# Windowed attention and a gated feed-forward in one kernel: which engine issues the transfers of results

## The chip, the cores and the metric

One core of one Trainium2 chip runs the whole program. The metric is the device time of one execution in microseconds (us), lower is better; the median of three runs stands for the kernel, and one further execution was taken with a profile.

## What is computed

Eight batches, eight heads, 512 local and 32 global positions, head size 64; then a feed-forward over 544 rows of 512 numbers per batch, with 1024 hidden ones:

```
out_g = softmax(q_g [k_g,k_l]^T / 8) [v_g,v_l]             # 32 global queries see everything
out_l = softmax(q_l [k_g, k_l where |i-j|<=32]^T / 8) [v_g,v_l]
x     = [out_g, out_l], heads side by side                  # 8 x 544 x 512
h     = max(x w_in, 0);  c = conv of 3 taps along the rows of h
out   = (h * sigmoid(c)) w_out
```

All inputs are float32 (the weights arrive as 64-bit numbers and are split on the chip into a high and a low part; x and the gated h are split too, and three products replace one).

## The kernel before

**Attention.** Heads go in pairs. `LQ` and `LV` load a pair's queries, keys and values (704 and 448 KB), `LG` the global queries. `SC` (line 258) makes the scores on TensorE in two PSUM banks, `MA` (286, 287) masks them and takes the maximum on VectorE, `EX` (299) exponentiates on ScalarE, `NP` normalizes, `TD` (309) transposes on VectorE, `PV` (350) multiplies by the values into four PSUM banks, and `UA` (205) copies these on ScalarE into a tile `nt`. Line 205 is the helper `cp` for every copy, line 208 the helper `sub` for every difference. The global queries run through `G`, `GM`, `GE`, `GS`, `GT`, `GC`, `GP` (436) and `GO`, which copies the result on ScalarE into a tile `og`.

**The row.** Results go to DRAM and come back in another shape: `XW` (line 361) writes `nt` into a DRAM tensor `row`, `GW` (448) writes `og` there, and `XR` (368) reads a piece of the row, 486 to 488 columns of one of four quarters of x, into a tile `xl`. `XH` (205, ScalarE) rounds it into `xh`, and `XL` (208, VectorE in the first chunk, GpSimd later) leaves the rest in `xl`. A piece needs every `XW` and `GW` whose columns lie in it.

**Feed-forward.** The row is cut into nine chunks (`CUTS`). For each, `Z` (466) makes eight tiles `ps_h` of hidden numbers, `RE`, `C1`, `C2`, `TH`, `GG`, `GH`, `GL` make the gate on ScalarE and VectorE, and `O` (520) makes four output tiles in `ps_o`. `OE` (205) copies one into a tile `o`, on ScalarE in the first chunk and on VectorE from the second on, and `ST` (534) stores it; where a chunk reaches over the end of a batch, `ST` is two transfers.

**Weights.** `WD` (168) loads eight pieces `raw` of 1 MB, and `WA` (107, ScalarE), `WC` (114 to 118 and 192, VectorE), `WH` (205, ScalarE), `WL` (208, VectorE) turn each into its two parts.

**Order.** A planner (`plan`, `arranged`) runs at build time: it has a cost and a due time for each operation and lists the operations in the order in which it would start them; `emit` records them in that order and ties each engine to it. So each engine, and each engine's queue of transfers, works strictly in the planner's order. In the planner's list of engines (`FIXED`, line 658) every transfer stands under SyncE (SP), and all are issued there. PSUM has eight banks for everything (`SLOTS["ps"]`), `nt`, `og` and `o` have two tiles each, `qk` four and `vf` six.

**Semaphores of transfers.** The framework deals eight semaphores, DMAHW0 to DMAHW7, in turn to the transfers of the whole program, whoever issues them. A transfer first waits for the landing of the last one that had its semaphore (where no other wait already covers that), so it waits for the eighth transfer before it.

Of the kernel before, what the change touches and what calls it, by code (L numbers as in the profile page):

```python
# [21 lines left out]
SL = 512  # L22
# [42 lines left out]
def attn_moe(ctx: ExitStack, tc: tile.TileContext, qk_d, vw_d, qg_d, w_in_d, w_out_d, cw_d, out_d):  # L65
    nc = tc.nc
# [24 lines left out]
    for b in range(4):  # L91
        rows = slice(b * SG, (b + 1) * SG)
        for k, sign in ((0, 1), (1, -1)):
            nc.gpsimd.affine_select(
                out=mask[rows, :, k], in_=mask[rows, :, k], pattern=[[0, 4], [sign, SG]], compare_op=ALU.is_ge, fill=NEG,
# [7 lines left out]
    row = dram.tile([NCT, P, NCOL], F32, name="row", bufs=1)  # L103
# [107 lines left out]
    heads = {}  # L211
# [146 lines left out]
    def XW(n):  # L358
        b, h = divmod(n, H)
        at = 1 + ROW * b + SG  # L360
        nc.sync.dma_start(out=row[h // 2, :, at : at + SL], in_=heads[n]["nt"])

    def XR(i):
        c, ct = divmod(i, NCT)
# [80 lines left out]

    def GW(n):
        at = ROW * (n // H)
        nc.sync.dma_start(
            out=row[:, :, at : at + 1 + SG].rearrange("c p q -> p c q"), in_=ogs[n // H % SLOTS["og"]]
        )  # L450

# [77 lines left out]
    def ST(o):  # L529
        c, mt = divmod(o, NCT)  # L530
        for b in range(B):
            lo, hi = max(CUTS[c], ROW * b), min(CUTS[c + 1], ROW * b + S)
            if lo < hi:
                nc.sync.dma_start(
                    out=out_d[b, mt, :, lo - ROW * b : hi - ROW * b], in_=outs[o][:, lo - CUTS[c] : hi - CUTS[c]]
                )

    emit(tc, B, dict(
        LQ=LQ, LV=LV, LG=LG, G=G, S=SC, M=MA, NM=NM, E=EX, NS=NS, NP=NP, TD=TD, P=PV, UA=UA, XW=XW, XR=XR,
        XH=XH, XL=XL,  # L540
        GM=GM, GE=GE, GN=GN, GS=GS, GT=GT, GC=GC, GP=GP, GO=GO, GW=GW,
        PZ=Z, RE=RE, C1=C1, Ca=lambda u: C2(u, 0), Cb=lambda u: C2(u, 2), TH=TH, GG=GG, GH=GH, GL=GL,
        Oa=lambda o: O(o, 0), Ob=lambda o: O(o, 1), OE=OE, ST=ST, WD=WD, WA=WA, WC=WC, WH=WH, WL=WL,
    ), phase)

# [431 lines left out]
```

## Time and profile before

| | us |
|---|---|
| runs (three) | 571.13, 573.1, 573.7 |
| median | 573.1 |
| the profiled execution, its own time | 569.44 |
| span of its instructions | 567.6 |

| engine | busy us | share of the span |
|---|---|---|
| TensorE, matmuls | 528.4 | 93% |
| TensorE, weight loads (beside the matmuls) | 442.8 | 78% |
| VectorE | 431.4 | 76% |
| ScalarE | 377.5 | 67% |
| GpSimd | 65.1 | 11% |

SP computes nothing. The time splits into two parts: until about 120 us weights are prepared, the first two batches' attention is made and TensorE has gaps; from there on TensorE is busy without a gap until the last chunk. The chain of work that ended last runs 82% of its length over TensorE and 11% over VectorE. Shares of the whole span hide this, so the stretches are to be read one by one.

### The profile page before, as it was taken

What the parts mean: (1) busy time and instruction counts of PE and PEld (TensorE: products, weight loads), DVE (VectorE), ACT (ScalarE), POOL (GpSimd) and SP (SyncE); (2) the same over time, 40 slices, a digit from 0 to 9 for tenths busy, and PEclk for the clock granted to TensorE, in tenths of its full rate; (3) what the DMA queues carried; (4) which work ended last, traced back from release to release, by engine and by line L of the source; (5) the groups of instructions that cost most, each with busy time, mean ns of one, the idle gap of its engine ahead of it and who ended that gap; (6) DMA issues with size and microseconds to landing.
All of it is one profiled execution on the core that took longest, in us unless ns stands there. A gap on an engine that the chain in (4) does not pass through costs nothing.

```text
span 567.6 us, 19439 instructions
## 1 busy us (share of the span) xinstructions
PE 528.4 (93%) x8208; PEld 442.8 (78%) x8208; DVE 431.4 (76%) x876; ACT 377.5 (67%) x1258; POOL 65.1 (11%) x73
## 2 busy tenths in 40 slices
PE   5574589889999999999999999999999999999997
PEld 4463468678888888888888888888888888888886
DVE  4889999987886798479847994699578873783771
ACT  4855787769974997399739973898489642441530
POOL 3400220110002001200120002000200040010000
PEclk9676689899999999999999999999999999999999
DMA  8879452464255333632464246333501321111001
GB/s 349 337 220 405 186 209 62 120 212 160 75 154 152 111 110 118 187 140 74 157 166 149 91 131 186 122 121 108 146 20 38 109 92 35 36 35 54 19 0 70
DMA packets 34982, 74.73 MB, mean 132 GB/s; under 512 B 9808, under 2 KB 21584, under 8 KB 33872
## 3 DMA queue, kind: packets, MB, share of 16 engines
q1 hardware_dynamic: 34896, 73.50, 39.0%
q8 instruction: 64, 1.05, 0.8%
q14 instruction: 22, 0.18, 0.1%
HBM read 55.65 MB, written 17.84 MB: 129 GB/s over the span
## 4 chain that ended last, share of the span: by engine, by line
PE 82%; DVE 11%; DMA 3%; ACT 2%; issue 2%; SPq 0%; ACTq 0%; DVEq 0%
PE ps_o L520 34%; PE ps_h L466 31%; PE ps_v L350 7%; PE ps_s L258 5%; PE go L436 3%; DVE negm L287 2%; DMA qgf<-qg 1%; DVE t L485 1%; DVE pt L309 1%; PE gt L421 1%; PE psg L280 1%; DVE ps_s L286 1%; DVE t L496 1%; DMA qk<-qk 1%; DVE wt L118 1%
## 5 line engine op out<-in xcount | busy, mean ns | idle before, releaser
L520 PE MATMUL ps_o<-g,w_out 128*128 128x484 f32 (+1 forms) x864 | 200.2, 385 | 2.1 <-ACT pgt L205 2.1
L466 PE MATMUL ps_h<-xh,w_in 128*128 128x486 f32 (+1 forms) x576 | 190.9, 395 | 1.5 <-ACT xh L205 1.5
L520 PEld LDWEIGHTS ps_o<-g,w_out 128*128 128x128 f32 x864 | 161.6, 189 | 30.8 <-issue 2.4
L466 PEld LDWEIGHTS ps_h<-xh,w_in 128*128 128x128 f32 x576 | 110.7, 192 | 22.8 <-ACT xh L205 2.6
L485 DVE SCALAR_TENSOR_TENSOR t<-h,cw,t 128x484 f32<-128x484 f32 (+1 forms) x144 | 105.9, 742 | 16.2 <-ACT t L238 15.6
L466 PE MATMUL ps_h<-xl,w_in 128*128 128x486 f32 (+1 forms) x288 | 112.1, 389 | 5.2 <-DVE xl L208 5.2
L299 ACT ACTIVATE pr<-ps_s,negm 128x128 f32<-128x128 f32 x256 | 90.3, 369 | 0.8
L208 POOL TENSOR_TENSOR xl<-xl,xh 128x486 fp32r<-128x486 f32 (+1 forms) x32 | 43.2, 1353 | 349.2 <-ACT xh L205 349.2
L474 ACT ACTIVATE h<-ps_h 128x486 f32<-128x486 f32 (+1 forms) x72 | 41.5, 577 | 46.1 <-PE ps_h L466 41.4
L350 PEld LDWEIGHTS ps_v<-pt,vf 32*64 32x64 f32 x3328 | 50.7, 140 | 20.8 <-issue 12.2
L466 PEld LDWEIGHTS ps_h<-xl,w_in 128*128 128x128 f32 x288 | 55.3, 192 | 14.3 <-DVE xl L208 6.0
L350 PE MATMUL ps_v<-pt,vf 32*64 32x64 f32 (+3 forms) x3328 | 56.6, 254 | 9.2 <-issue 4.4
L496 DVE SCALAR_TENSOR_TENSOR t<-t,h 128x484 f32<-128x484 f32 (+1 forms) x72 | 51.0, 713 | 16.5 <-ACT t L492 15.5
L492 ACT ACTIVATE t<-t 128x484 f32<-128x484 f32 (+1 forms) x72 | 43.8, 609 | 27.4 <-DVE t L485 27.4
L322 ACT ACTIVATE pr<-pr,sums 128x128 f32<-128x128 f32 x192 | 60.1, 404 | 0.6 <-DVE sums L316 0.5
L286 DVE TENSOR_TENSOR ps_s<-ps_s,mask 128x256 f32<-128x256 f32 x64 | 26.8, 418 | 38.8 <-PE ps_s L258 38.6
L238 ACT ACTIVATE t<-h,cw 128x484 f32<-128x484 f32 (+1 forms) x72 | 50.5, 703 | 4.8 <-DVE g L208 4.2
L299 ACT ACTIVATION_READ_ACCUMULATOR pr<-ps_s,negm 128x1 f32 x256 | 53.1, 208 | 0.0
L258 PE MATMUL ps_s<-qk 64*32 64x128 f32 x2048 | 39.6, 298 | 14.0 <-DMA qk<-qk 11.8
L309 DVE STREAM_TRANSPOSE pt<-pr 128x512 f32<-128x512 f32 x64 | 44.4, 701 | 10.4 <-ACT pr L322 9.9
L208 DVE TENSOR_TENSOR g<-t,g 128x484 fp32r<-128x484 f32 (+1 forms) x72 | 49.6, 692 | 1.4
L258 PEld LDWEIGHTS ps_s<-qk 64*32 64x32 f32 x2048 | 32.2, 114 | 21.6 <-issue 7.4
(63 smaller groups left out, 414.5 us busy)
## 6 DMA issues: line engine op xcount, KB each, us to landing
qk<-qk SPq DMA_DIRECT2D x32, 704.0 KB, 5.5
vf<-vw SPq DMA_DIRECT2D x32, 448.0 KB, 4.0
row<-nt SPq DMA_DIRECT2D x32, 256.0 KB, 3.8
xl<-row SPq DMA_DIRECT2D x24, 243.0 KB, 3.3
raw<-w_in SPq DMA_DIRECT2D x4, 1024.0 KB, 12.3
raw<-w_out SPq DMA_DIRECT2D x4, 1024.0 KB, 9.9
xl<-row SPq DMA_DIRECT2D x8, 244.0 KB, 3.1
out<-o SPq DMA_DIRECT2D x4, 242.0 KB, 3.5
```

What stands on the lines that cost most here:

```text
L208: eng(key).tensor_tensor(out=out, in0=in0, in1=in1, op=ALU.subtract)
L238: nc.scalar.activation(out=out, in_=in_, func=AF.Copy, scale=by)
L258: nc.tensor.matmul(heads[n + j]["s"][b * SG : (b + 1) * SG, t].rearrange("p (a b k) -> p a b k", a=2, b=2), lhsT=qk[rows, at : at + SG], r ...
L299: nc.scalar.activation(out=st["p"][:, t, :], in_=st["s"][:, t, :], func=AF.Exp, scale=SCALE, bias=st["m"][:, t : t + 1], accum_out=two["r" ...
L309: nc.vector.transpose(out=st["pt"][:, n % 2].rearrange("p t k q -> p (t k q)"), in_=heads[n]["p"].rearrange("p t k -> p (t k)"))
L322: nc.scalar.activation(out=p[:, t], in_=p[:, t], func=AF.Copy, scale=r[:, t : t + 1])
L350: nc.tensor.matmul(x, lhsT=v, rhs=p, start=k == 0, stop=k == len(work[j, b]) - 1)
L466: nc.tensor.matmul(st["z"][:, 0:n], lhsT=w[:, ft, ct, :], rhs=x, start=i == 0, stop=i == 3 * NCT - 1)
L485: nc.vector.scalar_tensor_tensor(out=st["t"], in0=st["h"][:, k : k + n], scalar=cw[:, 3 * ft + k : 3 * ft + k + 1], in1=st["t"], op0=ALU.m ...
L492: nc.scalar.activation(out=t, in_=t, func=AF.Tanh)
L496: nc.vector.scalar_tensor_tensor(out=t, in0=t, scalar=1.0, in1=h, op0=ALU.add, op1=ALU.mult)
L520: nc.tensor.matmul(ps, lhsT=w[:, mt, ft, :], rhs=g, start=ft + i == 0, stop=ft == NFT - 1 and i == 2)
```

## The change

Three calls in the kernel's text change their engine. The tables of the planner stay as they are: it still counts these transfers as SP's, gives them no time on ScalarE, and sets the same start times.

```diff
     def XW(n):
...
-        nc.sync.dma_start(out=row[h // 2, :, at : at + SL], in_=heads[n]["nt"])
+        nc.scalar.dma_start(out=row[h // 2, :, at : at + SL], in_=heads[n]["nt"])
...
     def GW(n):
         at = ROW * (n // H)
-        nc.sync.dma_start(
+        nc.scalar.dma_start(
             out=row[:, :, at : at + 1 + SG].rearrange("c p q -> p c q"), in_=ogs[n // H % SLOTS["og"]]
         )
...
     def ST(o):
...
-                nc.sync.dma_start(
+                nc.scalar.dma_start(
                     out=out_d[b, mt, :, lo - ROW * b : hi - ROW * b], in_=outs[o][:, lo - CUTS[c] : hi - CUTS[c]]
                 )
```

In the built program 104 of 221 transfers leave SP for ScalarE: 32 `XW`, 8 `GW` and 64 of `ST`. The other instructions keep their order on every engine.

**ScalarE, the first chunk's pieces and weights.** `nt_822` is the result of the fourth pair of heads of the first batch; `wt` are weights in work, `xl_875` the first piece of the row. Before:

```order
L205 COPY nt_822<-ps_v_731 128x128
L205 CAST w_in0_118<-wt_718 128x1024 [waits DVE_49]
L107 ACTIVATE wt_865<-raw_424 128x1024 [waits DMAHW4_49,DVE_49]
L107 ACTIVATE wt_872<-raw_500 128x1024 [waits DMAHW5_49]
L238 ACTIVATE negm_867<-negm_867 128x4 [waits DVE_49]
L299 ACTIVATE pr_884,sums_885<-ps_s_788,negm_867 128x128 [waits PE_49,Activation_49,Pool_49]
L299 ACTIVATE pr_884,sums_885<-ps_s_788,negm_867 128x128 x3
L205 CAST xh_874<-xl_875 128x486 [waits DMAHW1_49]
```

Now:

```order
L205 COPY nt_822<-ps_v_731 128x128
L205 CAST w_in0_118<-wt_718 128x1024 [waits DVE_49]
L107 ACTIVATE wt_865<-raw_424 128x1024 [waits DVE_49]
L361 DMA row_114<-nt_822 128x512 [waits DMAHW1_49,Activation_49]
L107 ACTIVATE wt_872<-raw_500 128x1024 [waits DMAHW5_49]
L238 ACTIVATE negm_867<-negm_867 128x4 [waits DVE_49]
L299 ACTIVATE pr_884,sums_885<-ps_s_788,negm_867 128x128 [waits PE_49,Activation_49,Pool_49]
L299 ACTIVATE pr_884,sums_885<-ps_s_788,negm_867 128x128 x3
L205 CAST xh_874<-xl_875 128x486 [waits DMAHW0_49]
```

The write of `nt_822` now stands in ScalarE's stream ahead of a weight piece, four exponentials and the rounding of `xl_875`, and it waits for semaphore DMAHW1.

**SP, the same place of the program.** Before:

```order
L223 DMA qk_726<-qk 128x1408 [waits DMAHW4_49,PE_49]
L448 DMA row_114<-og0_126 128x4x33 [waits DMAHW5_49,Activation_49,Pool_49]
L230 DMA vf_786<-vw 128x896 [waits DMAHW6_49,PE_49]
L230 DMA vf_828<-vw 128x896 [waits DMAHW7_49,PE_49]
L361 DMA row_114<-nt_822 128x512 [waits DMAHW0_49,Activation_49]
L368 DMA xl_875<-row_114 128x486 [waits DMAHW5_49,DMAHW1_49]
L223 DMA qk_877<-qk 128x1408 [waits DMAHW2_49]
```

Now:

```order
L223 DMA qk_726<-qk 128x1408 [waits DMAHW1_49,PE_49]
L230 DMA vf_786<-vw 128x896 [waits DMAHW5_49,PE_49]
L230 DMA vf_828<-vw 128x896 [waits DMAHW6_49,PE_49]
L368 DMA xl_875<-row_114 128x486 [waits DMAHW7_49,DMAHW2_49,DMAHW0_49]
L223 DMA qk_877<-qk 128x1408 [waits DMAHW1_49]
```

The two writes are gone from SP's queue. `qk_726`, then `qk_877`, and then (on ScalarE) the write of `nt_822` are the holders of DMAHW1, one after the other: the write waits until `qk_877` has landed. Before, it waited for `vf_327`, a load of the program's start.

**ScalarE, a store in the running part.** `o_3982` is an output tile of the third chunk. Now:

```order
L299 ACTIVATE pr_3963,sums_3897<-ps_s_3805,negm_3902 128x128 x4
L238 ACTIVATE negm_3907<-negm_3907 128x4
L534 DMA out<-o_3982 128x121 [waits DMAHW5_49,DVE_49]
L534 DMA out<-o_3982 128x362 [waits DMAHW6_49]
L299 ACTIVATE pr_3988,sums_3926<-ps_s_3839,negm_3907 128x128 [waits Activation_49]
L299 ACTIVATE pr_3988,sums_3926<-ps_s_3839,negm_3907 128x128 x3
```

Before, the two middle rows stood on SP and nothing else was different here. They wait for VectorE's copy of the tile, and four exponentials stand behind them.

## Rows read from the trace of the kernel before

**Rows 1.** Busy time by stretch of the span. Columns: stretch, its length, then busy us and (count) of TensorE's matmuls, its weight loads, VectorE, ScalarE, GpSimd; TensorE's granted clock; mean share of the DMA engines; GB/s.
```profile
40.00:60.00 20.00, 9.95 (x249) 6.96 (x233) 19.08 (x29) 12.80 (x30) 1.55 (x2) 0.67 1.01 379
60.00:80.00 20.00, 15.57 (x103) 11.87 (x103) 19.48 (x34) 14.21 (x56) 6.68 (x6) 0.79 0.30 112
80.00:100.00 20.00, 19.14 (x290) 16.15 (x291) 19.59 (x54) 15.70 (x41) 1.34 (x1) 0.91 0.40 144
100.00:120.00 20.00, 15.79 (x484) 13.21 (x483) 17.40 (x26) 13.90 (x34) 3.29 (x2) 0.91 0.45 126
...
200.00:300.00 100.00, 100.00 (x1813) 84.44 (x1813) 75.45 (x165) 72.59 (x249) 10.88 (x8) 1.00 0.45 136
300.00:400.00 100.00, 100.00 (x1626) 83.65 (x1628) 80.06 (x182) 82.53 (x294) 6.83 (x5) 1.00 0.41 130
```

**Rows 2.** Waits of SP's queue, line and who ended them: us in total, times, longest us.
```profile
SPq L534 <- DVE o L205: 152.7, 27, 28.0
...
SPq L361 <- ACT nt L205: 49.6, 21, 11.5
...
SPq L448 <- ACT og L205: 11.6, 8, 4.5
```

**Rows 3.** SP's issues in order of time: start, time that the issue took (from the first's start to the last's end where there are several), line, transfer, count. Left out are all between.
```profile
25.18 0.33 SPq L361 DMA_DIRECT2D row<-nt  x1
...
37.77 0.38 SPq L448 DMA_DIRECT2D row<-og  x1
...
248.55 0.82 SPq L534 DMA_DIRECT2D out<-o  x2
...
260.94 0.82 SPq L534 DMA_DIRECT2D out<-o  x2
...
365.32 0.82 SPq L534 DMA_DIRECT2D out<-o  x2
...
377.68 0.82 SPq L534 DMA_DIRECT2D out<-o  x2
```

**Rows 4.** Pieces of the chain that ended last: start, length, what. A DMA's length runs from its issue to its landing.
```profile
0.74 4.25 DMA qk<-qk
...
37.77 3.27 DMA row<-og
...
41.49 0.52 SPq L223
```

**Rows 5.** TensorE in order of time: start, length, line, operation and tiles, shapes, count, and in brackets the idle time ahead and what ended it.
```profile
32.49 2.52 PE L436 MATMUL go<-pgt,vf 128*64 128x32 f32 x78 [0.58 <-DVE pgt L205]
...
49.35 3.68 PE L258 MATMUL ps_s<-qk 64*32 64x128 f32 x128 [6.82 <-DMA qk<-qk]
```

**Rows 6.** ScalarE in order of time, the same columns, in the place where the first piece of the row is rounded.
```profile
37.45 0.26 ACT L205 COPY og<-go 128x128 f32<-128x128 f32 x1
...
41.49 2.24 ACT L107 ACTIVATE wt<-raw 128x1024 f32<-128x1024 f32 x2
43.64 0.19 ACT L238 ACTIVATE negm<-negm 128x4 f32<-128x4 f32 x1
...
45.20 0.21 ACT L299 ACTIVATION_READ_ACCUMULATOR pr<-ps_s,negm 128x1 f32 x1
47.47 0.60 ACT L205 CAST xh<-xl 128x486 fp32r<-128x486 f32 x1 [2.05 <-DMA xl<-row]
```

**Rows 7.** VectorE in order of time, the same place.
```profile
46.51 1.22 DVE L192 SCALAR_TENSOR_TENSOR wt<-raw,wt 128x1024 uint32<-128x1024 uint32 x1
48.10 0.67 DVE L208 TENSOR_TENSOR xl<-xl,xh 128x486 fp32r<-128x486 f32 x1 [0.36 <-ACT xh L205]
```

**Rows 8.** Transfers by kind, on the page: count, KB each, median us from issue to landing.
```profile
vf<-vw SPq DMA_DIRECT2D x32, 448.0 KB, 4.0
row<-nt SPq DMA_DIRECT2D x32, 256.0 KB, 3.8
```

**Rows 9.** ScalarE in order of time, behind the places of two stores in the third chunk (248 and 261 us) and in the fifth (365 and 378 us), and the end of the last exponential ahead of `PV`, for each.
```profile
248.71 0.37 ACT L299 ACTIVATE pr<-ps_s,negm 128x128 f32<-128x128 f32 x1
...
261.11 0.36 ACT L299 ACTIVATE pr<-ps_s,negm 128x128 f32<-128x128 f32 x1
...
266.28 0.20 ACT L299 ACTIVATION_READ_ACCUMULATOR pr<-ps_s,negm 128x1 f32 x1
...
365.48 0.37 ACT L299 ACTIVATE pr<-ps_s,negm 128x128 f32<-128x128 f32 x1
...
377.86 0.36 ACT L299 ACTIVATE pr<-ps_s,negm 128x128 f32<-128x128 f32 x1
...
383.02 0.20 ACT L299 ACTIVATION_READ_ACCUMULATOR pr<-ps_s,negm 128x1 f32 x1
```

**Rows 10.** TensorE in order of time: `PV` behind those exponentials, and the last gap before the full stretch.
```profile
116.97 0.31 PE L350 MATMUL ps_v<-pt,vf 32*64 32x32 f32 x6 [1.82 <-issue]
...
267.15 1.57 PE L350 MATMUL ps_v<-pt,vf 32*64 32x128 f32 x104
...
383.88 1.57 PE L350 MATMUL ps_v<-pt,vf 32*64 32x128 f32 x104
```

**Rows 11.** Waits of ScalarE: who ended them, us in total, times, longest us.
```profile
ACT h L474 <- PE ps_h L466: 41.4, 23, 11.2
```

**Rows 12.** ScalarE: the rounding of a piece of the second chunk.
```profile
125.20 0.60 ACT L205 CAST xh<-xl 128x486 fp32r<-128x486 f32 x1 [2.16 <-DMA xl<-row]
```

## The prediction, made before the changed kernel ran

> **What bounds the kernel now.** I read the stretches first, then SP's waits, then the places to which the diff moves something. The reader is to see in the stretches that there are two regimes [rows 1]. From 40 to 100 us VectorE is busy 19.08, 19.48 and 19.59 of each 20 us while TensorE has gaps: there VectorE's list is what must not be delayed. From 200 to 400 us TensorE is busy 100.00 of 100 at a granted clock of 1.00; ScalarE is busy 72.59 and 82.53. There a change can give nothing unless it makes matmuls fewer or shorter, and costs only what opens a gap on TensorE.
>
> In SP's waits the eye falls on 152.7 us at `ST`, 49.6 us at `XW` and 11.6 us at `GW` [rows 2]. They are the time that loads stand behind transfers of results in SP's queue, and the change removes all of it. But a wait on SP costs only if somebody waits for the load behind it, and in the full stretch TensorE waits for nothing [rows 1]. So this most visible row buys nothing behind 120 us. It can buy something only in the start, where TensorE once waits 6.82 us for a load, `qk` [rows 5].
>
> **Term 1: the start.** On SP the `GW` at 37.77 us stands ahead of two `vf` loads; behind it come the first pieces of the row and the load of `qk_877`, which is issued at 41.49 us and ends TensorE's wait at 49.35 us [rows 3, 4, 5]. The piece needs the landing of `GW`, 37.77 + 3.27 = 41.04 us [rows 4]. ScalarE's copy of `og` ends at 37.45 + 0.26 = 37.71 [rows 6], so ScalarE issues `GW` at the same time as SP did, and the piece and `qk_877` leave no earlier than now, at about 41.1 and 41.5. What does leave earlier are the two `vf` loads: they need only the values' buffers, which `GP` frees at 32.49 + 2.52 = 35.0 us [rows 5]; with the median landing of 4.0 us [rows 8] they are in at about 39 and no longer share the DMA engines (1.01, that is full, in this stretch [rows 1]) with `qk_877`. A `qk` load of the program's start took 4.25 us [rows 4], so `qk_877` lands at T = 41.49 + 4.25 = 45.7 instead of 49.2. Alone that would be a gain.
>
> It is not alone, for ScalarE's write of `nt_822` now holds the same semaphore behind `qk_877` and waits for T, and behind it in ScalarE's stream stand `wt_872`, `negm` and four exponentials and then the rounding of `xl_875`. Before, the two `wt` took from 41.49 to 43.73 (2.24 us for two), so ScalarE is at the write at about 42.7, and the rest, from 42.6 to the end of the exponentials at 45.4, is 2.8 us [rows 6]. With an issue of 0.33 to 0.38 us [rows 3]: 45.7 + 0.35 + 2.75 = 48.8, and the rounding's 0.60 us [rows 6] ends at 49.4. VectorE's `XL` began at 48.10 [rows 7] and now begins at 49.4. VectorE, which is behind the bound of this stretch, stands at that point and its whole list moves: **+1.3 us**. Bounds: nothing if T is 44.4 or earlier (then the rounding ends at 48.1 as before), and if `qk_877` lands as late as now, 49.3, the same sum gives 53.0, that is +4.9. I take 1.3, since the row nearest to a load with free DMA engines is the 4.25.
>
> **Term 2: the stores.** An output tile that crosses a batch's end is stored by two transfers, and SP's issue of such a pair takes 0.82 us, four of them in the third and fifth chunks, from 248.55, 260.94, 365.32 and 377.68 us [rows 3]. Each now lies between ScalarE's instructions. ScalarE would go on at 248.71, 261.11, 365.48 and 377.86 [rows 9], so the pairs delay it by 249.37 - 248.71 = 0.66, then 0.65, 0.66 and 0.64 us: 1.31 per chunk. `PV` begins 0.67 us behind the last exponential in either place (266.48 to 267.15, 383.22 to 383.88) [rows 9, 10]. I read this as the lead that ScalarE has: up to 0.67 us the delay is swallowed, beyond it TensorE stops, 1.31 - 0.66 = 0.65 us. The fourth chunk has a pair of this kind as well, so three periods: **+2.0 us**. Bounds: nothing, if ScalarE catches up in between; 3 x (2 x 0.82 - 0.66) = 2.9 if the whole issue falls on it.
>
> [...]
>
> The other stores fall where ScalarE waits for TensorE anyhow (`ps_h`, 41.4 us over 23 waits) [rows 11]: nothing, as long as these waits are there; without that cover each would cost its 0.33 to 0.41.
>
> **Term 3: the writes of the running part.** An `XW` stands right behind ScalarE's own copies and needs no other engine; its issue of 0.33 us [rows 3] is covered by the same waits for `ps_h` [rows 11]: 0, at most what three uncovered ones would be, 1.0. Its wait for the eighth transfer before it is short, since these have had several us and land in 3.8 to 4.0 [rows 8]. One place has no cover: the piece of the second chunk for which ScalarE waits 2.16 us until 125.20 [rows 12]. There a write of 256 KB now runs beside loads instead of ahead of them. At 379 GB/s [rows 1] 256 KB are 0.7 us; nothing if the queue's order was the limit; I take **+0.3**, as the write shares the engines with two others.
>
> **Sum.** 1.3 + 2.0 + 0.3 = +3.6 us. On the profiled execution's own time, 569.44, this is 573.0; the median of the three runs is 3.7 us above that execution, so I put the sum on the median: 573.1 + 3.6 = **576.7 us**. What the measurement of this kernel can tell from no change is about 0.5%, 2.9 us, so the lines lie at 570.2 and 576.0.
>
> **Rivals.**
>
> *Swallowed* (not slower by the bound). ScalarE may still have earlier instructions at work while its sequencer issues the stores, or the lead of 0.67 us may be refilled between two pairs. For: a pair stands behind four exponentials that take 1.3 us, and 0.16 us of it is covered even by the plain sum [rows 3, 9]. Against: the store waits for VectorE's copy, which ends only 0.16 us before ScalarE would go on. Then term 2 is nothing and 1.3 remains: 574.4. [...]
>
> *Dear* (slower by more). `qk_877` lands as late as now, because the loads that leave SP earlier are followed by others that fill the same engines, and the pairs cost in full: 4.9 + 2.9 + 0.7 = +8.5, **581.6**. For: DMA engines at 1.01 from 40 to 60 us [rows 1]. Against: the two `vf` are the only big loads between, and they go 3 us earlier.
>
> *Nothing*. The waits of SP go and nobody had waited for them; the issues hide in ScalarE's 17 to 27 idle us per 100 [rows 1]; the wait for T is short: 573.1. [...]
>
> *Faster*. SP runs ahead, so that loads are early in the start. VectorE's idle time from 40 to 100 us is 60 - 19.08 - 19.48 - 19.59 = 1.85 us [rows 1], and the last gap of TensorE ahead of the full stretch is 1.82 us at 116.97 [rows 10]; if both go, -3.7: 569.4. The point from which it decides: T below 44.4 us, and no other write of ScalarE's held by a landing. Against: nearly all that VectorE does there waits for itself, and the gap of 1.82 is an issue, not a wait for a transfer.
>
> **How the numbers follow.** Forecast 0.40 (own range 576.0 to 579); swallowed 0.33; dear 0.12; nothing 0.08; faster 0.07. Slower by over 0.5%: 0.40 + 0.12 = 0.52; within: 0.33 + 0.08 = 0.41; faster: 0.07. The forecast is close to its line, at +3.6 against 2.9, which makes the first two chances nearly even. The range takes in the forecast, swallowed, nothing and the dear case's sum: 571.5 to 581.6, the lower end 1.6 us under no change, for a part of the start's gain without its wait.
>
> **What would show it.** Term 1: in ScalarE's stream around 42.7 us a gap that the landing of `qk` ends near 45.7, and VectorE's `XL` at about 49.4 instead of 48.10; TensorE's first wait for `qk` shorter by 3.5 us. Term 2: ScalarE idle by about 0.65 us at each of the pairs, and a gap of about 0.65 us on TensorE ahead of `PV`, three times. Term 3: ScalarE's rounding behind the wait at 125.20 later than the shift of term 1 explains. In SP's waits the rows of `ST`, `XW` and `GW` must be gone. I am wrong if TensorE stays full from 120 us on and the time is up all the same, if ScalarE's gaps at the pairs are there and TensorE shows none (swallowed), or if the first chunk begins earlier than now.

## The result, and the profile after

| | before | changed |
|---|---|---|
| median, us (16 runs each, same chip) | 572.27 | 575.15 |
| range of the runs, us | 570.64 to 575.01 | 572.9 to 578.12 |
| ratio, with its 95% interval | | 1.0065 [1.0048, 1.0082] |
| profiled execution, own time / span, us | 569.44 / 567.6 | 575.57 / 573.8 |

By the ratio the change costs 0.65%, or 0.0065 x 572.3 = 3.7 us (2.7 to 4.7); the two medians lie 2.9 us apart. The forecast was slower, +3.6 us on 573.1, a ratio of 1.0063. The two profiled executions lie 6.1 us apart, more than the medians, because the one of before was faster than any of its 16 runs here; so a second trace of before was taken (e5 below), and shifts are given against both where it matters.

**The start.** Four views of the changed kernel in the place of [rows 3 to 7]. First ScalarE's stream (start, length, what, idle time ahead and its end):

```profile
38.09 0.26 ACT L205 COPY og<-go 128x128 f32<-128x128 f32 x1
38.38 0.38 ACTq L448 DMA_DIRECT2D row<-og  x1
...
42.12 1.18 ACT L107 ACTIVATE wt<-raw 128x1024 f32<-128x1024 f32 x1
48.01 0.34 ACTq L361 DMA_DIRECT2D row<-nt  x1
48.39 1.17 ACT L107 ACTIVATE wt<-raw 128x1024 f32<-128x1024 f32 x1 [5.08 <-DMA qk<-qk]
49.45 0.20 ACT L238 ACTIVATE negm<-negm 128x4 f32<-128x4 f32 x1
...
51.12 0.60 ACT L205 CAST xh<-xl 128x486 fp32r<-128x486 f32 x1
```

SP's queue:

```profile
13.24 1.46 SPq L230 DMA_DIRECT2D vf<-vw  x2
16.25 2.12 SPq L223 DMA_DIRECT2D qk<-qk  x2
...
42.30 0.33 SPq L368 DMA_DIRECT2D xl<-row  x1
42.68 0.90 SPq L223 DMA_DIRECT2D qk<-qk  x2
```

TensorE, and then VectorE:

```profile
29.99 1.97 PE L350 MATMUL ps_v<-pt,vf 32*64 32x128 f32 x79
32.87 0.67 PE L350 MATMUL ps_v<-pt,vf 32*64 32x96 f32 x25 [0.92 <-issue]
...
48.07 3.66 PE L258 MATMUL ps_s<-qk 64*32 64x128 f32 x128 [4.15 <-DMA qk<-qk]
```

```profile
51.75 0.67 DVE L208 TENSOR_TENSOR xl<-xl,xh 128x486 fp32r<-128x486 f32 x1 [2.64 <-ACT xh L205]
```

ScalarE stands for 5.08 us at the write of `nt_822`, and the wait ends with the landing of `qk`, a transfer that the write has nothing to do with but the semaphore. TensorE gets `qk_877` 1.3 us earlier than before (48.07 against 49.35 [rows 5]), which helps nobody: VectorE's `XL` is at 51.75 instead of 48.10 [rows 7], and its busy time from 40 to 60 us falls from 19.08 [rows 1] to 16.16. (The first row below is of this stretch, the other two belong to the running part.)

```profile
40.00:60.00 20.00, 10.02 (x276) 6.92 (x267) 16.16 (x21) 10.30 (x22) 0.42 (x1) 0.76 0.83 307
...
200.00:300.00 100.00, 99.59 (x1742) 83.94 (x1724) 77.86 (x171) 74.54 (x261) 8.13 (x7) 1.00 0.44 134
300.00:400.00 100.00, 99.81 (x1568) 83.10 (x1566) 76.82 (x179) 80.63 (x295) 7.53 (x6) 1.00 0.40 129
```

VectorE does not make this up. A weight operation of line 192, 60 us later, before and then changed, is late by 3.64 us, as `XL` was by 3.65:

```profile
108.89 2.12 DVE L192 SCALAR_TENSOR_TENSOR wt<-raw,wt 128x1024 uint32<-128x1024 uint32 x1
```

```profile
112.53 2.12 DVE L192 SCALAR_TENSOR_TENSOR wt<-raw,wt 128x1024 uint32<-128x1024 uint32 x1
```

**The running part.** TensorE is no longer at 100.00 there. Where I had put the gaps, there are none: at the two pairs of stores of the third chunk ScalarE idles 0.76 and 0.35 us, and `PV` (before at 267.15 [rows 10]) follows without a gap on what precedes it, 0.20 us ahead of the end of the last exponential. ScalarE's and TensorE's streams:

```profile
252.94 0.83 ACTq L534 DMA_DIRECT2D out<-o  x2
253.82 0.37 ACT L299 ACTIVATE pr<-ps_s,negm 128x128 f32<-128x128 f32 x1 [0.76 <-DVE sums L315]
...
265.48 0.59 ACT L474 ACTIVATE h<-ps_h 128x488 f32<-128x488 f32 x1
265.56 0.82 ACTq L534 DMA_DIRECT2D out<-o  x2
266.43 0.37 ACT L299 ACTIVATE pr<-ps_s,negm 128x128 f32<-128x128 f32 x1 [0.35 <-DVE g L205]
...
271.54 0.22 ACT L299 ACTIVATION_READ_ACCUMULATOR pr<-ps_s,negm 128x1 f32 x1
```

```profile
271.24 0.39 PE L466 MATMUL ps_h<-xh,w_in 128*128 128x488 f32 x1
271.56 1.57 PE L350 MATMUL ps_v<-pt,vf 32*64 32x128 f32 x104
...
290.62 0.87 PE L350 MATMUL ps_v<-pt,vf 32*64 32x128 f32 x46
291.80 0.89 PE L350 MATMUL ps_v<-pt,vf 32*64 32x64 f32 x58 [0.32 <-issue]
...
441.58 0.46 PE L350 MATMUL ps_v<-pt,vf 32*64 32x128 f32 x12
442.20 1.38 PE L350 MATMUL ps_v<-pt,vf 32*64 32x128 f32 x92 [0.16 <-ACT pr L299]
```

Two other kinds of gap are there instead. At 291.49 TensorE stops for 0.32 us inside a `PV` with no engine or transfer shown that it waits for ("issue"), and at 442.04 for 0.16 us for ScalarE's exponentials, late by pairs of stores. In SP's waits the rows of `ST`, `XW` and `GW` [rows 2] are gone, as the change says; the largest sum is now that of the pieces for a write of `nt` (columns as in [rows 2]):

```profile
SPq L368 <- DMA row<-nt: 121.1, 22, 35.5
```

### The profile page after: what moved, and what is told of

Its sections match the earlier page's. It is cut to its first block, busy times and chain, and to the rows that moved or that the text cites. A ratio compares the mean times of both kernels' runs of the same rounds, so it can differ in the third digit from the quotient of the medians.

```text
span 573.8 us, 19410 instructions
## 1 busy us (share of the span) xinstructions
PE 532.8 (93%) x8208; PEld 445.2 (78%) x8208; DVE 431.6 (75%) x876; ACT 376.6 (66%) x1258; POOL 64.5 (11%) x73
## 3 DMA queue, kind: packets, MB, share of 16 engines
q8 instruction: 64, 1.05, 0.8%
## 4 chain that ended last, share of the span: by engine, by line
PE 74%; DVE 12%; DMA 7%; ACT 4%; issue 1%; SPq 0%; ACTq 0%; DVEq 0%
PE ps_o L520 30%; PE ps_h L466 29%; PE ps_v L350 7%; PE ps_s L258 4%; PE go L436 3%; DMA row<-nt 2%; DVE negm L287 2%; DMA qk<-qk 2%; DMA vf<-vw 1%; DVE ps_s L286 1%; DVE t L485 1%; DMA xl<-row 1%; DVE pt L309 1%; PE psg L280 1%; DVE t L496 1%
## 5 line engine op out<-in xcount | busy, mean ns | idle before, releaser
L474 ACT ACTIVATE h<-ps_h 128x486 f32<-128x486 f32 (+1 forms) x72 | 41.5, 578 | 40.0 <-PE ps_h L466 21.7
L350 PE MATMUL ps_v<-pt,vf 32*64 32x64 f32 (+3 forms) x3328 | 58.3, 257 | 8.3 <-issue 3.2
L208 DVE TENSOR_TENSOR g<-t,g 128x484 fp32r<-128x484 f32 (+1 forms) x72 | 51.5, 717 | 1.4
```

Source lines behind the costliest of these rows:

```text
L208: eng(key).tensor_tensor(out=out, in0=in0, in1=in1, op=ALU.subtract)
L350: nc.tensor.matmul(x, lhsT=v, rhs=p, start=k == 0, stop=k == len(work[j, b]) - 1)
```

## The experiments

**Theory A**: the loss is the wait of the write of `nt_822` and what stands behind it on ScalarE. **Rival B**: the start differs by chance, and the loss is made behind 120 us, by the stores or by the second queue. Later letters are added where the runs asked for them: **D**, loads that run ahead of the first writes; **S**, a lead that swallows each pair of stores; rival **E**, the late landing of the write of `nt_822` itself.

Ratios are over the kernel before, timed beside it on the same chip. "XL" is the start of VectorE's first `XL`, 48.10 and 48.39 us in the two traces of before, 51.75 in the changed kernel.

| | what is on ScalarE | ratio [95%] | XL |
|---|---|---|---|
| e1 | all but the write of `nt_822` | 1.0023 [0.9999, 1.0046] | 48.97 |
| e2 | `GW` | 1.0010 [0.9989, 1.0032] | 48.02 |
| e3 | `XW` | 1.0084 [1.0053, 1.0115] | 53.25 |
| e4 | `ST` | 1.0001 [0.9981, 1.0021] | 47.85 |
| e6 | all but the first batch's `XW` | 1.0024 [1.0001, 1.0048] | 48.92 |
| e7 | the first three `XW` | 1.0009 [0.9986, 1.0032] | 48.33 |
| e8 | the write of `nt_822` | 1.0066 [1.0042, 1.0089] | 51.24 |
| e9 | all, that write behind the first rounding | 1.0053 [1.0028, 1.0077] | 48.38 |
| e10 | all, each `XW` right behind its copies | 1.0131 [1.0107, 1.0156] | 53.80 |
| e11 | `ST`, in twice as many transfers | 1.0469 [1.0434, 1.0503] | 47.69 |
| e12 | as e9, `ST` on SP | 1.0014 [0.9990, 1.0037] | 48.47 |

**e1, one write back on SP.**

```diff
-        nc.scalar.dma_start(out=row[h // 2, :, at : at + SL], in_=heads[n]["nt"])
+        (nc.sync if n // 2 == 3 else nc.scalar).dma_start(out=row[h // 2, :, at : at + SL], in_=heads[n]["nt"])
```

> The change with one write put back: the write of nt_822 (fourth pair of the first batch) is issued by SP again, ahead of the first piece; all other transfers stay with ScalarE. In the changed kernel ScalarE waited 5.08 us for qk_877 at this write and VectorE's XL began at 51.75 instead of 48.10. Theory A (that wait is the larger part of the loss): XL within 0.8 us of 48.1, and the time falls by 1 to 3 us against the change, to a ratio of 1.001 to 1.004 over the kernel before. Rival B (the shift in the start is chance of these two executions, the granted clock from 28 to 42 us being 0.80 and 0.76 in one and 0.50 and 0.56 in the other; the loss is made behind 120 us): the ratio stays at 1.005 to 1.008.

103 of the 104 transfers stay moved, and most of the loss is gone; XL is late by 0.9 us against the first trace of before, 0.6 against the second. The ratio is in theory A's range, and XL is 0.1 us outside its own, taken from the first trace.

**e2, e3, e4, one part each** (each diff is one of the change's three hunks).

> Only the eight writes of global results (GW) go to ScalarE. In the changed kernel the PV behind GP, in which a GW is issued, took 1.70, 2.01 and 1.90 us at 232, 291 and 349 us instead of 1.50. Theory A1 (a GW issued by ScalarE starves TensorE of instructions by itself): the same three PV at 1.7 to 2.0, ratio 1.001 to 1.003. Rival A2 (it takes more transfers on the second queue, the writes of nt beside loads): PV at 1.50, ratio 1.000 within 0.002. Rival B: no difference. The start has no wait of ScalarE here, so XL is at 48.1 within 0.8 us in all.

> Only the 32 writes of pair results (XW) go to ScalarE. Theory A: the write of nt_822 stands ahead of the exponentials; if it waits for the landing of qk_877 again, XL at 50 to 52 us, ratio 1.003 to 1.007. Theory A2: PV behind GP at 1.7 to 2.0 us as in the changed kernel. Rival B: ratio below 1.002, since the pairs of stores are not on ScalarE.

> Only the 64 stores go to ScalarE. The prediction's term 2: +2.0 us, ratio 1.0035, with TensorE gaps ahead of PV at about 267, 325 and 384 us. Theory A: ScalarE is late by 0.65 us at the pairs, but TensorE takes it up except in the last attention chunk (0.3 to 0.7 us at 424 to 442 us): ratio 1.000 to 1.002.

`XW` alone makes the whole loss, the stores none that can be measured. e3 lies above its range in both, 1.0084 and 53.25: the wait is 6.5 us there, since `GW` stays on SP, the `vf` loads leave no earlier and `qk_877` lands only 7.4 us after its issue. In e4 TensorE loses at the two places in the last attention chunk, and at no pair before:

```profile
435.75 0.46 PE L350 MATMUL ps_v<-pt,vf 32*64 32x128 f32 x12
436.38 1.38 PE L350 MATMUL ps_v<-pt,vf 32*64 32x128 f32 x92 [0.17 <-ACT pr L299]
```

That `PV` takes 437.69 - 435.75 = 1.94 us from its first matmul to the next group's, against 1.50 in both traces of before; the `SC` at 424 us takes 1.35 against 1.09. So +0.70 us at the two places together, and in all six kernels with whole stores on ScalarE (the change, e1, e4, e6, e9, e10) 0.67 to 0.98, in the others 0.00. The expectation of e2 on stretched `PV` was not decided: two of its three were stretched, but e4, without any `GW` on ScalarE, has such too.

**e5, the kernel before once more.**

> The kernel before, unchanged, for a second trace. Theory C (its profiled execution was one without a dip of TensorE's clock at 118 us, which e1, e2 and e3 had, at 0.54 to 0.78): the second trace has times within 0.3 us of the first up to 110 us, and may differ by up to 2 us at 118 to 124 us by the granted clock alone. The same PV as before are stretched or others, by 0.2 to 0.6 us, if those stretches are chance.

571 us, span 569.0. VectorE's `XL` is within 0.3 us of the first trace, but TensorE is 2.1 us late at 121 us and 1.7 us at 131 us, and that is made between 113 and 121 us. The two stretches from 113 us in the first trace, then in this one (columns as in [rows 1]):

```profile
113.00:117.00 4.00, 2.18 (x128) 2.02 (x125) 2.81 (x3) 2.54 (x6) 1.22 (x1) 1.00 0.45 135
117.00:122.00 5.00, 5.00 (x145) 4.12 (x145) 3.75 (x8) 3.38 (x17) 0.00 (x0) 1.00 0.66 200
```

```profile
113.00:117.00 4.00, 1.89 (x115) 1.73 (x112) 2.76 (x4) 3.88 (x7) 0.70 (x1) 1.00 0.44 145
117.00:122.00 5.00, 4.47 (x78) 3.69 (x78) 4.57 (x8) 2.90 (x14) 0.51 (x1) 0.72 0.56 155
```

The granted clock there is 1.00 in one execution of the same program and 0.72 on average in the other; ahead of it TensorE had been busy for 2.18 and 1.89 of 4 us, and no run shows what sets the clock. Twelve matmuls of `O` take 4.46 us there instead of 2.89. I had expected up to 2 us of this kind. A single pair of traces cannot be subtracted at their ends, and 6.1 us between two profiled executions don't contradict 3.7 us by the ratio.

**e6 and e7, the loads that run ahead.** e6 puts the writes with `n < 8` back on SP; e7 is the kernel before with only the first three writes (`n < 6`) on ScalarE.

> The change with the four writes of the first batch's pairs (XW, n below 8) on SP again; all GW, all stores and 28 XW stay with ScalarE. Theory A+D (the loss is made in the start: 3 us by the wait of nt_822's write, 0.66 us by four loads that run ahead of the first three writes and fill the DMA engines): nothing late at 30 us, XL at 48.1 within 0.3 us, the four loads issued at 25.5 to 33 us again, ratio 0.999 to 1.002. Rival (the 28 XW of the running part cost too): ratio above 1.003 with TensorE losing over 1.5 us behind 130 us.

> Only the first three writes of nt go to ScalarE; the fourth and all the rest stay on SP. Theory D (loads run ahead): SP issues vf, vf, qk, qk at about 13, 14, 16 and 18 us instead of 25.6 to 32.8, the first write lands at about 32 us instead of 28, TensorE stops inside the PV at 26 and 30 us for want of instructions, VectorE at 30 us is late by 0.66, XL at 48.7 to 49.0; ratio 1.000 to 1.003. Rival (the 0.66 comes from the clock): nothing late at 30 us.

In e7 SP, then TensorE, then VectorE:

```profile
13.96 1.45 SPq L230 DMA_DIRECT2D vf<-vw  x2
16.35 2.76 SPq L223 DMA_DIRECT2D qk<-qk  x2
```

```profile
30.05 1.77 PE L350 MATMUL ps_v<-pt,vf 32*64 32x128 f32 x79
33.48 0.46 PE L350 MATMUL ps_v<-pt,vf 32*64 32x96 f32 x25 [1.65 <-issue]
```

```profile
30.69 0.18 DVE L114 TENSOR_SCALAR cw<-cw 128x24 f32<-128x24 f32 x1 [3.41 <-ACT cw L107]
```

Before, the same instruction of VectorE began at 29.98 (0.71 earlier), and the four loads were issued from 25.56 to 32.84 us, each behind a write. Now they leave 12 to 14 us early, into engines that are still full (share 1.01 from 24 to 28 us, 1.02 in the changed kernel, 0.50 before), and TensorE stops in an "issue" of 1.65 us. The pages of before and of the changed kernel list a queue of instructions among the DMA queues ("q8 instruction: 64, 1.05, 0.8%"); that TensorE lacks instructions and that the loads hold them up is a guess from that line, which no run shows. XL is at 48.33, under the expected 48.7: the lateness is made up, and the ratio shows no loss. Theory D is right that the loads run ahead and that VectorE is late at 30 us, and wrong on what that is worth. In e6 the loads wait again and VectorE is on time at 30 us, but XL is at 48.92, not within 0.3 us as expected, and the ratio of 1.0024 is a little above its range: TensorE has such a stop there too, 0.80 us inside the `PV` at 29.54, and 0.30 us even in e5. So such stops come without the early loads as well, only shorter.

**e8, that one write alone.**

```diff
-        nc.sync.dma_start(out=row[h // 2, :, at : at + SL], in_=heads[n]["nt"])
+        (nc.scalar if n // 2 == 3 else nc.sync).dma_start(out=row[h // 2, :, at : at + SL], in_=heads[n]["nt"])
```

> Only the write of nt_822 goes to ScalarE: one transfer of 221. It waits there for the semaphore that qk_877 holds. GW stays on SP, so the vf loads are no earlier and qk_877 lands at 48 to 49.3 us as before. Theory A: ScalarE waits 5 to 6.5 us, XL at 51.5 to 53.0 instead of 48.1, ratio 1.005 to 1.009: one transfer makes as much as the whole change. Rival (VectorE's lateness is made up before 120 us): XL late but ratio below 1.003.

ScalarE and VectorE of e8:

```profile
41.65 1.16 ACT L107 ACTIVATE wt<-raw 128x1024 f32<-128x1024 f32 x1
47.50 0.34 ACTq L361 DMA_DIRECT2D row<-nt  x1
47.89 1.14 ACT L107 ACTIVATE wt<-raw 128x1024 f32<-128x1024 f32 x1 [5.08 <-DMA qk<-qk]
```

```profile
51.24 0.67 DVE L208 TENSOR_TENSOR xl<-xl,xh 128x486 fp32r<-128x486 f32 x1 [3.33 <-ACT xh L205]
```

One transfer of 221 gives 1.0066, the whole change 1.0065. XL is 0.3 us under its range, as `qk_877` lands at 47.4 instead of 48 or later. With e1, which puts the same one back, this settles which transfer makes the larger part of the loss. That it does so by its place in ScalarE's stream is what the next runs ask; none of them changes the semaphore alone.

**e9 and e10, the write later and earlier in ScalarE's stream.** Both keep the whole change. e9 issues it behind the rounding of `xl_875`, e10 issues every write right behind its copies.

```diff
     def XW(n):
-        b, h = divmod(n, H)
+        if n != 6:
+            write(n)
+
+    def write(n):
+        b, h = divmod(n, H)
...
     def XH(i):
         cp("XH", xs[i][0], f(xs[i][1]))
+        if i == 0:
+            write(6)
```

> The whole change, with one instruction moved in ScalarE's stream: the write of nt_822 now stands behind the rounding of xl_875 instead of ahead of wt_872, negm, the four exponentials and that rounding. It still goes out from ScalarE and still waits for the semaphore of qk_877. Theory A (what costs is what stands behind the waiting write): XL at 48.4 to 49.0 instead of 51.75, ratio 1.001 to 1.003, as in e1, although the write leaves no earlier. Rival (the write itself is late for the piece that reads it, or the second queue costs): ratio stays at 1.005 or above.

> The whole change, with every write of nt issued right behind the four copies that make it. In the start the write of nt_822 then stands ahead of a cast of w_in (1.05 us) and one more wt (1.15 us) too, and waits for the same semaphore. Theory A: XL later than in the change by up to 2.2 us, at 52.8 to 54.0, ratio 1.008 to 1.012. Rival (a write that is issued earlier helps the row's pieces): ratio below 1.0065.

In e9 the write goes out at the same time as in the changed kernel, with the same semaphore and from the same engine, and VectorE waits no more. ScalarE, VectorE:

```profile
45.94 0.61 ACT L205 CAST xh<-xl 128x486 fp32r<-128x486 f32 x1
47.81 0.34 ACTq L365 DMA_DIRECT2D row<-nt  x1
48.50 1.05 ACT L205 CAST w_in<-wt 128x1024 fp32r<-128x1024 f32 x1 [1.96 <-DVE wt L192]
```

```profile
48.38 0.66 DVE L208 TENSOR_TENSOR xl<-xl,xh 128x486 fp32r<-128x486 f32 x1
```

The stall is gone as expected, but the time is a miss: 1.0053 where 1.001 to 1.003 was expected, and 1.005 or above was the rival's; its interval, 1.0028 to 1.0077, holds both. In e10 the stall takes 7.34 us and XL stands at 53.80, as expected; the ratio of 1.0131 is a little above the range.

**e11, twice as many stores.**

```diff
-                nc.scalar.dma_start(
-                    out=out_d[b, mt, :, lo - ROW * b : hi - ROW * b], in_=outs[o][:, lo - CUTS[c] : hi - CUTS[c]]
-                )
+                for h in (slice(0, 64), slice(64, 128)):
+                    nc.scalar.dma_start(
+                        out=out_d[b, mt, h, lo - ROW * b : hi - ROW * b], in_=outs[o][h, lo - CUTS[c] : hi - CUTS[c]]
+                    )
```

> As e4 (only the stores on ScalarE), and each store cut into two halves of 64 partitions, so that 128 transfers are issued and a pair becomes four issues, about 1.6 us instead of 0.82. Theory S (each pair is swallowed by a lead of about 0.7 us at PV, and only what is beyond shows): TensorE stops by 0.3 to 1.0 us ahead of PV in each of the chunks from 250 to 400 us and by 1.3 us or more at 424 to 442 us; ratio 1.004 to 1.008. Rival (ScalarE's earlier instructions run on while its sequencer issues): gaps only at 424 to 442 us, ratio below 1.003.

ScalarE at the second pair of the third chunk, and TensorE:

```profile
270.86 2.42 ACTq L535 DMA_DIRECT2D out<-o  x4
273.32 0.37 ACT L299 ACTIVATE pr<-ps_s,negm 128x128 f32<-128x128 f32 x1 [1.94 <-DMA out<-o]
```

```profile
271.67 1.21 PE L280 MATMUL psg<-qk,qgf 64*32 64x384 f32 x48
274.88 0.49 PE L466 MATMUL ps_h<-xh,w_in 128*128 128x488 f32 x1 [2.00 <-ACT pr L299]
```

The dose was larger than meant: a half of 64 partitions takes 0.47 to 0.61 us to issue, so four take 2.42 us, not 1.6. And the answer is steep: 0.82 us at this place cost TensorE nothing, 2.42 cost it 2.0 (a part of it is left over from the four issues of the chunk's first pair); over the kernel it is +27 us instead of 0. So ScalarE's stream has a lead, and what exceeds it stops TensorE. How much of the 27 us is that is not shown: elsewhere single issues took up to 1.84 us (at 207.96; 2.07 in the changed kernel), more than the halves here. The rival (issues run beside ScalarE's own work) falls as an account of the whole, though 0.5 us of this issue too runs beside an activation.

**e12, as e9 with the stores on SP.**

> As e9 (the write of nt_822 behind the rounding), and the stores on SP again. In all traces with stores on ScalarE the two places at 424 and 436 us lost 0.24 to 0.55 and 0.43 to 0.47 us, in none without. Theory A: XL at 48.1 to 49.0 and no loss at those two places; ratio 1.000 to 1.003. Rival E (e9's ratio of 1.0053 comes from the write itself, which left at 47.81 and landed only at 56.62, so that a piece and two weights behind it are late): ratio at 1.004 or above, with the loss ahead of 120 us.

1.0014, XL at 48.47, and the two places at 424 and 436 us are back at 1.09 and 1.50. Theory A's range holds. e12 has all of e3's moved writes (and `GW`, which costs nothing measurable in e2): with the write of `nt_822` behind the rounding they cost 0.9990 to 1.0037, ahead of it (e3) 1.0053 to 1.0115. So it is the place in ScalarE's stream that costs, and rival E falls as the larger part. The write lands late in e9 and e12 too, and the piece that needs it leaves SP at 56.63 and 54.56 us instead of 49.23, but VectorE is no more than 0.34 us late at the same operation of line 192 (e9, then e12; before 108.89):

```profile
109.17 2.13 DVE L192 SCALAR_TENSOR_TENSOR wt<-raw,wt 128x1024 uint32<-128x1024 uint32 x1
```

```profile
109.23 2.14 DVE L192 SCALAR_TENSOR_TENSOR wt<-raw,wt 128x1024 uint32<-128x1024 uint32 x1
```

What stays open is why e9's runs are slower than e12's. The two differ in the stores alone, and in the traces TensorE stands at the same times in both within 0.1 us from 60 to 230 us and 0.65 us later at the end in e9, about the loss at 424 and 436 us; the ratios differ by 0.4%, 2.2 us, and their intervals overlap. No version tried beats the kernel before.

## Why the prediction was right, step by step

**The sum** was +3.6 and +3.7 was measured, but that the two agree is luck: the first term was too small and the second too large by about the same. The direction was right, and so was the place of the larger loss. One of my own signs of being wrong came true, ScalarE's gaps at the pairs with none on TensorE.

**Term 1, the wait of `nt_822`'s write**: right place, right mechanism, wrong size. Predicted: T at 45.7, XL at 49.4, +1.3. Found: the write issued at 48.01, XL at 51.75, +3.65 against the first trace and +3.4 against the second; TensorE's wait for `qk` is 4.15 us, shorter by 2.7 and not by 3.5. The single transfer of e8 makes 1.0066, 3.8 us. Everything behind T was sized well: 0.34 us for the issue, then 51.12 - 48.39 = 2.73 us, against the 2.75 of the sum. The failed step is T itself, 45.7, where the load landed at about 48.0. Two numbers failed in it. The load left at 42.68 instead of 41.5, because the `og` copy ended 0.6 us later (the lateness at 30 us, e7) and `GW` took about 3.9 us to land (38.38 to the piece's issue at 42.30) instead of 3.27. And it landed 5.3 us after its issue (42.68 to 48.01), not in the 4.25 of the program's start. My reason for 4.25 was that the `vf` loads would be in; they were, and it counts: from issue to landing `qk_877` took 5.0 to 6.0 us in the seven traces with `GW` on ScalarE and 6.1 to 8.1 in the seven without. But SP issues `qk_890`, a load of the same size, in the same 0.90 us, which I didn't look at; that the two share the engines is the likely rest, and no run takes it away. The bounds, 0 to 4.9, held it.

**Term 2, the stores**: the delays at the pairs were there (0.76 and 0.35 us of idle time), but TensorE didn't pay them. Predicted 2.0 us ahead of `PV` in three chunks; found 0.7 us in one, the last of the attention, and e4's ratio is 1.0001. Two steps failed. The first is the adding of two pairs to 1.31 us. Measured against TensorE's own shift between the two traces, ScalarE is 0.72 us late behind the first pair of the third chunk, 0.45 ahead of the second, 0.92 behind it and 0.85 at the last exponential ahead of `PV`, and the same within 0.1 in the fourth and fifth: it gives a part back between the pairs, and at the second 0.5 us of the issue run beside an activation that is still at work (265.48 to 266.07). The second is the lead, which I read as 0.67: `PV` starts at 271.56 while that exponential ends at 271.76, and in the last chunk TensorE stops for it only behind twelve matmuls of `PV` (442.04), so the lead is larger than the distance I read, and at least the 0.85 us that cost nothing. This was the rival "swallowed", in both of its forms, though the lead is only in part refilled. That ScalarE's next activation waits for the end of the issue, which the sum took for granted, is so at both pairs of the third chunk: it starts 0.05 us after the issue, 253.82 after 253.77 and 266.43 after 266.38. What the sum got wrong is what the engine still has in hand, and that is what the price hangs on.

**Term 3, the running part**: predicted 0.3 us at one place; that place was as before but for the shift of 4 us (129.26 for 125.20, behind a wait of 2.24 us for 2.16). What I didn't see is the `PV` that stops in an "issue" (0.32 us at 291.49). The four `PV` behind a `GP` (at 228, 286, 344 and 403 us) are 0.6 and 0.3 us over 4 x 1.50 in the two traces of before, 1.6 in the changed one, and 0.8 to 1.6 in the four others with all or nearly all on ScalarE (e1, e6, e9, e10). With the stores on SP (e12) they are 1.4, with one part alone 0.5 to 1.2. That this is the second queue is likely, but the spread is as large as the effect: argued, not shown.

**The rivals.** "Dear" was nearer at the start (a late `qk_877`, 49.3 for the 48.0 found), but not at the stores. "Nothing" is right that SP's time bought nothing here. But e8 shows what it leaves out: on ScalarE a transfer's own wait becomes the wait of all that stands behind it, 5.08 us there. "Faster" fell with its condition, T below 44.4.

## What to carry to other kernels

Before a transfer is moved to an engine that computes, look at what it will wait for there, its semaphore's last holder included, and at what stands behind it on that engine; the place in the stream counts more than the number of transfers (1 of 104 made the loss). Here an issue on an engine with a lead cost nothing as long as the lead covered it (0.82 us), and a much longer one stopped the engine that waits (2.42 us of issue, 2.00 us of TensorE). So lead and lateness are to be read at each place: two delays add up only as far as the first has not been given back by then (0.92 us here, not 1.31), and the lead ends where the waiting engine needs the result, not where its first instruction starts (at 442.04 TensorE stopped only behind twelve matmuls of `PV`). And a queue that is freed runs ahead (12 to 14 us in e7): look at what its early loads will collide with.

## What the runs showed of the hardware

- Issues on ScalarE took about as long as on SP (changed kernel against before): a pair of stores mostly 0.82 us on both, a write of `nt` 0.33 on both, one of `og` 0.38 and 0.37 (medians), the longest single store 2.07 and 1.85. Halves of 64 partitions took longer than whole stores, 0.47 to 0.61 us each (e11) against a median of 0.35.
- With four loads let loose into DMA engines at a share of 1.01 TensorE stopped in an "issue" of 1.65 us inside one `PV` (e7), 0.92 us in the changed kernel; without them it was 0.30 (e5) and 0.80 us (e6).
- The 704 KB of `qk_877` took 5.0 to 6.0 us from issue to landing where two `vf` loads had left at 34 to 36 us (5.3 in the changed kernel), and 6.1 to 8.1 where they left at 38 to 40 (7.7 before).
- The granted clock at 117 to 122 us differed between executions of one program, 1.00 (first trace of before) and 0.72 (e5); twelve matmuls took 2.89 and 4.46 us.
